# Where the folds of the next search and routing's small steps stand in VectorE's order: top-k attention into a mixture of experts

## The chip, the cores and the metric

The kernel runs on one core of one Trainium2 chip. The metric is the device time of one execution in microseconds, as the median of several runs. The engines are named as in the profile: PE is TensorE (PEld its weight loads), DVE is VectorE, ACT is ScalarE, POOL is GpSimd, SP is SyncE, which issues most DMAs.

## The reference

Attention for 8 batches of 8 heads with 576 tokens of 64 values, in which each query keeps only its 32 largest scores; then a mixture of 8 experts with one expert for each token.

```python
# attention: q, k, v are (8, 8, 576, 64) float32
scores = scale * np.matmul(q, k.transpose(0, 1, 3, 2))
kth = np.partition(scores, -32, axis=-1)[..., -32:-31]
scores = np.where(scores >= kth, scores, -1e9)
attn = np.exp(scores - max); attn = attn / (attn.sum(-1, keepdims=True) + 1e-09)
x = np.matmul(attn, v)          # then (B, H, S, D) -> (4608, 512)
# experts: w_gate (512, 8), w1 (8, 512, 1024), w2 (8, 1024, 512)
logits = x @ w_gate
expert = np.argmax(logits, axis=1)
gate = 1 / (exp(logits - max).sum(-1) + 1e-09)      # the probability of the chosen one
y = np.maximum(x @ w1[expert], 0) @ w2[expert]
out = gate[:, None] * y
```

## The kernel before

**Slots.** The work is 144 slots, 18 for each batch. A slot holds two tiles of 128 queries by 576 scores, lying side by side in one buffer `s` as 128 x 2 x 2 x 288. In `loop()` the order of PE, ACT and DVE is that of the program's text (a manual schedule for these three engines), and most POOL instructions are kept in program order by `in_turn`. PE multiplies the scores of slot i four slots ahead, ACT copies them to `s` three ahead (L306).

**The search.** For the 32nd largest score of a row DVE does not scan all 576 scores. It first folds them. `fold` makes h, the larger of the two halves (L313, 288 values for each of the two tiles), and l, the smaller (L315). `fold_on` folds h again: the larger quarter goes to `few` (L321), the smaller to `hl`. In `lists` (L350) the 8 largest of l and of the two halves of hl are put behind the 144 values of few. `search` then runs four rounds, in each of which MAX8 takes the next 8 largest of each tile (L372) and MATCH_REPLACE8 strikes them out (L382). What can have been missed is noted in `doubt` (L399), and a slow exact path behind the main loop would be taken if it mattered.

**When the folds come.** Slot i searches what was folded in slot i-1. Its text first folds s of slot i+1 to h and l, then runs its own search. `fold_on` for slot i+1 comes later, as a function `then` that `search` calls: in most slots ahead of the last round, in a quiet slot behind the second round's maxima. A slot is quiet if its number is between 1 and 47 and no rows, scatters or stores have been put on POOL (`k.crowded`). In a quiet slot hl is not made by DVE but by two integer operations of POOL (L326, L327: larger + smaller - larger).

**Behind the search.** ACT makes `low` from the 32nd value (L393), then w, a ReLU with a very steep slope, in two halves (`depths`, L409). POOL subtracts it from the scores (`less`, L418, two instructions of 128 x 576 that read s and w), and then makes `doubt`. ACT takes the exponential of w later in the slot (`weights`, L426). PE transposes w one slot later (`transposed`, L437, with ACT's copies L444), and multiplies by v in `outputs` (L474) when a unit of two heads is whole.

**Routing's small steps.** A batch's routing is spread over the slots behind it as generators: `divisors` (one reciprocal, L503, of what ACT has just put into rz), `choice` (L535 to L545), `places` (L570 to L579), `filled_up` and `table` (L642 to L677). Each yields after one small DVE instruction. They wait in the list `aside`. `tick()` runs one step of the first of them; `search` calls it in its third and fourth rounds, after each MAX8 and each MATCH_REPLACE8, which is six places a slot. `through(steps)` runs what is left of one before its result is needed. On POOL routing puts `logits` (L511 to L516), `rows` (L525, 128 x 640) and the scatters of finished rows to `x_rows` in DRAM (L590). `ending` is the generator that walks a unit through these places; `at_place(name)` moves it on.

**Experts.** Blocks of 128 rows of one expert are fetched (SP queue: rows L797, weights L789 and L791), and their matmuls (L942, L959) are cut into pieces that are mixed into the slots by a credit. What is left of them runs on PE when the slots are done. Before that `fill_up` writes empty rows behind each expert's last row, from the SBUF tile `blank`, which also fills nine blocks of `x_rows` at the start (L993).

Of the kernel before, what the change touches and what calls it, by code (L numbers as in the profile page):

```python
# [9 lines left out]
F32 = mybir.dt.float32  # L10
I32 = mybir.dt.int32
AF = mybir.ActivationFunctionType
ALU = mybir.AluOpType
# [31 lines left out]
def kernel(  # L45
# [47 lines left out]
    nc = tc.nc  # L93
    B, U, P, _ = qk.shape
    N, Dm = out.shape
    S = N // B
    E = moe_w_gate.shape[1]
# [6 lines left out]
    HF = S // 2  # L104
    QF = S // 4
# [5 lines left out]
    XW = Dm + 2  # L111
# [3 lines left out]
    CAP = N + P  # L115
# [125 lines left out]
    w1v = moe_w1.rearrange("e (dt p) f -> p e dt f", p=P)  # L241
    w2v = moe_w2.rearrange("e (ft p) d -> p e ft d", p=P)
    xv = x_rows.rearrange("(r p) w -> p r w", p=P)
    blank = const.tile([P, XW], F32, name="blank")
    nc.gpsimd.memset(blank[:, 0:Dm + 1], 0.0)
    nc.gpsimd.iota(blank[:, Dm + 1:XW].bitcast(I32), pattern=[[0, 1]], base=N, channel_multiplier=0)
    scattered, fetched, fills = [], [], []

    def groups(u):
# [4 lines left out]
    def in_turn(put):  # L254

        if not k.exact:
            tc.keep_in_program_order(put)
        return put
# [47 lines left out]
            lambda m=m, ps=ps: nc.scalar.copy(s[:, m, :, :], ps[:, :, 0:HF]) for m, ps in enumerate(got)  # L306
        ]

    def fold(s):

        f = SimpleNamespace()
        f.h = k.att.tile([P, 2, HF], F32, name="h", bufs=1)
        nc.vector.tensor_tensor(f.h, s[:, :, 0, :], s[:, :, 1, :], op=ALU.max)  # L313
        f.l = k.att.tile([P, 2, HF], F32, name="l")
        nc.vector.tensor_tensor(f.l, s[:, :, 0, :], s[:, :, 1, :], op=ALU.min)  # L315
        return f

    def fold_on(f, aside_too=False):

        f.few = k.att.tile([P, 2, LW], F32, name="few", bufs=3)  # L320
        nc.vector.tensor_tensor(f.few[:, :, 0:QF], f.h[:, :, 0:QF], f.h[:, :, QF:HF], op=ALU.max)  # L321
        hl = k.att.tile([P, 2, QF], I32, name="hl", bufs=1)
        f.hl, f.aside = hl[:, :, :].bitcast(F32), aside_too
        if aside_too:
            one, other, more = (a.bitcast(I32) for a in (f.h[:, :, 0:QF], f.h[:, :, QF:HF], f.few[:, :, 0:QF]))
            in_turn(nc.gpsimd.tensor_tensor(hl, one, other, op=ALU.add))  # L326
            in_turn(nc.gpsimd.tensor_tensor(hl, hl, more, op=ALU.subtract))  # L327
        else:
            nc.vector.tensor_tensor(f.hl, f.h[:, :, 0:QF], f.h[:, :, QF:HF], op=ALU.min)

    aside = []

    def tick():

        while aside:
            if next(aside[0], "end") != "end":
                return
            aside.pop(0)

    def through(steps):  # L340
        for _ in steps:
            pass
        if steps in aside:
            aside.remove(steps)

    def lists(f):

        for m in range(2):
            for j, away in enumerate((f.l[:, m, :], f.hl[:, m, 0:QF // 2], f.hl[:, m, QF // 2:QF])):
                nc.vector.max(out=f.few[:, m, QF + 8 * j:QF + 8 * j + 8], in_=away)  # L350

    def search(tiles, s, f, then=lambda: None, soon=False):

        m_all = range(2)
        tops = k.small.tile([P, 2, TOP_K], F32, name="tops", bufs=4)
        if k.exact:
            src = [s[:, m, :, :].rearrange("p j k -> p (j k)") for m in m_all]
            width = S
        else:
            src = [f.few[:, m, 0:QF] for m in m_all]  # L360
            width = LW
            if not f.aside:
                lists(f)
        scr = k.att.tile([P, 2, width], F32, name="scr", bufs=1)
        nbias = k.small.tile([P, 2], F32, name="nbias", bufs=3)
        R = TOP_K // 8

        for r in range(R):
            if r == R - 1 and not soon:
                then()  # L370
            for m in m_all:
                nc.vector.max(out=tops[:, m, r * 8:(r + 1) * 8], in_=src[m])  # L372
                if r > 1:
                    tick()
            if r == 1 and soon:
                then()
            if r == 0:
                in_turn(nc.gpsimd.tensor_scalar_mul(nbias, tops[:, :, 0], -scale))
            if r < R - 1:
                for m in m_all:  # L380
                    first = r == 0 and not k.exact
                    nc.vector.match_replace(  # L382
                        out=src[m] if first else scr[:, m, :], in_to_replace=tops[:, m, r * 8:(r + 1) * 8],
                        in_values=src[m], imm_value=NEG,
                    )
                    if r > 1:
                        tick()
                    src[m] = f.few[:, m, :] if first else scr[:, m, :]
                if first and f.aside:
                    lists(f)  # L390
        thr = tops[:, :, TOP_K - 1]
        low = k.small.tile([P, 2], F32, name="low", bufs=3)
        nc.scalar.activation(low, thr, AF.Copy, scale=STEEP)  # L393

        def doubts():
            n, i = tiles[0]
            at = n.b * U + n.u
            over = doubt[:, at:at + 2, 2 * NC, :] if tails(tiles) else doubt[:, at, 2 * i:2 * i + 2, :]
            k.last_pool = in_turn(nc.gpsimd.tensor_tensor(  # L399
                over, f.few[:, :, QF + 7:LW:8], _inner(thr, NL), op=ALU.subtract  # L400
            )).ins

        return low, nbias, doubts
# [583 lines left out]
    with fast:  # L987
        units = [(b, u) for b in range(B) for u in range(U)]
        unit.append(load_unit(*units[1]))
        for n in unit:  # L990
            load_values(n)
        for r in [e * CAP for e in range(E)] + [EMPTY * P]:
            nc.sync.dma_start(x_rows[r:r + P, :], blank)  # L993

        work = [(b, g) for b in range(B) for u in range(0, U, 2) for g in groups(u)]
        per_batch = len(work) // B
# [77 lines left out]
        def ending(b, u):  # L1074
# [15 lines left out]
            div = divisors(n)  # L1090
            next(div)
            aside.append(div)
            yield "products"
            next(out_steps)
            if b * U + u + 2 < len(units):
# [98 lines left out]
        def loop():  # L1194
# [5 lines left out]
                    step()  # L1200
            multiply(AHEAD)
            f_of[0] = fold(s_of[0])
            fold_on(f_of[0])
            for i, (b, g) in enumerate(work):
                tiles = tiles_of(i)
                u, tile = g[0]
                if tile == 0 and u % 2 == 0:
                    open_unit(tiles[0][0])
                if tails(tiles):
                    open_unit(tiles[1][0])  # L1210

                then, quiet = lambda: None, 0 < i < QUIET and not k.crowded
                if i + 1 < len(work):
                    f_of[i + 1] = fold(s_of[i + 1])
                    then = lambda: fold_on(f_of[i + 1], quiet)
                low, nbias, doubts = search(tiles, s_of[i], f_of.pop(i), then, quiet)
                k.crowded = False
                at_place("small")
                w_of[i] = depths(s_of[i], low)
                less(s_of.pop(i), w_of[i])  # L1220
                doubts()
                at_place("pool")
                at_place("relu")
                at_place("rows")
                put_stores()
                scatter(1)
                at = i % per_batch
                if at == FIRST and b:
                    rate = level(b) * PIECES / (U * NT)
                credit += rate * len(g)  # L1230
                room = left
                if b == B - 1 and at >= ARRIVED:
                    room -= KEEP
                    credit = room / (len(work) - i)
                share = {0: 0.5, 1: 1.2, 2: 1.6, 3: 0.5, 2 * NC: 1.4}[tile]
                now = max(0, min(int(credit * share + 0.5), room))
                credit -= now
                clock = i
                if i + AHEAD < len(work):
                    s_of[i + AHEAD], steps = scores(got_of.pop(i + AHEAD))  # L1240
                    for step in steps:
                        step()
                evacuate()
                at_place("turn")
                turns = turning(i - 1) if i else iter(())
                next(turns, None)
                part = min(BETWEEN, now - now // 2)
                rest = pieces(part)
                next(turns, None)
                rest = pieces(now - now // 2 - part + rest)  # L1250
                weights(tiles, w_of[i], nbias)
                next(turns, None)
                evacuate()
                if i + AHEAD + 1 < len(work):
                    multiply(i + AHEAD + 1)
                if tile == NC - 1:
                    end = ending(b, u)
                    late.append([end, next(end)])
                at_place("products")
                at_place("weights")  # L1260
                credit = min(credit + pieces(now // 2 + rest), 6 * rate)
# [149 lines left out]
```

## Time and profile before

| what | value |
| --- | --- |
| median of 3 runs | 1316.55 us (1310.98 to 1316.97) |
| the profiled execution's own time | 1312.35 us |
| its span, first to last instruction | 1310.7 us |
| mean granted TensorE clock | 0.969 |
| busy: PE, PEld | 1184.7 us (90%), 830.4 us (63%) |
| busy: DVE | 1064.8 us (81%), 4587 instructions |
| busy: ACT, POOL | 931.8 us (71%), 715.4 us (55%) |
| DMA | 220.95 MB, 169 GB/s over the span |

How to read the lines of the prediction. The busy slices cut the span into 40 equal parts, a digit being the busy share in tenths. A stretch has its bounds, its length, then busy time and number of instructions for PE, PEld, DVE, ACT and POOL, the granted clock, the share of the DMA engines and GB/s. A group has line, engine, operation, output<-input, shapes and count, then busy time in all and mean ns of one, then the engine's idle time ahead of it and what ended it. In the order of time a line begins with the start and the duration in us. "Waits" that the profile names are those on semaphores: an instruction that has been issued and stands still for another reason shows only as a long one.

### The profile page before, as it was taken

What the parts mean: (1) busy time and instruction counts of PE and PEld (TensorE: products, weight loads), DVE (VectorE), ACT (ScalarE), POOL (GpSimd) and SP (SyncE); (2) the same over time, 40 slices, a digit from 0 to 9 for tenths busy, and PEclk for the clock granted to TensorE, in tenths of its full rate; (3) what the DMA queues carried; (4) which work ended last, traced back from release to release, by engine and by line L of the source; (5) the groups of instructions that cost most, each with busy time, mean ns of one, the idle gap of its engine ahead of it and who ended that gap; (6) DMA issues with size and microseconds to landing.
All of it is one profiled execution on the core that took longest, in us unless ns stands there. A gap on an engine that the chain in (4) does not pass through costs nothing. (4 is left out here: it accounts for less than half of the span.)

```text
span 1310.7 us, 24598 instructions
## 1 busy us (share of the span) xinstructions
PE 1184.7 (90%) x7654; PEld 830.4 (63%) x7654; DVE 1064.8 (81%) x4587; ACT 931.8 (71%) x2136; POOL 715.4 (55%) x867
## 2 busy tenths in 40 slices
PE   5776676899889989999999999999999999999995
PEld 3443343666566556666666666767666777699973
DVE  7999999999999999999999999999999943000000
ACT  4888877898888888988888887898878851111210
POOL 4777766777755575658564745576558542000000
PEclk9778988999999999999999999999999999999998
DMA  5000112741474147534745554448454549986680
GB/s 150 30 30 30 31 38 90 278 165 39 142 267 137 47 158 283 175 110 159 291 174 183 161 217 174 165 149 283 147 199 158 209 161 295 386 298 213 219 286 19
DMA packets 98509, 220.95 MB, mean 169 GB/s; under 512 B 5181, under 2 KB 25917, under 8 KB 98368
## 3 DMA queue, kind: packets, MB, share of 16 engines
q1 hardware_dynamic: 91664, 199.02, 43.9%
q0 software_dynamic: 6416, 19.97, 4.3%
q8 instruction: 62, 1.02, 0.3%
q14 instruction: 79, 0.65, 0.2%
q10 hardware_dynamic: 288, 0.30, 0.1%
HBM read 195.88 MB, written 24.17 MB: 168 GB/s over the span
## 5 line engine op out<-in xcount | busy, mean ns | idle before, releaser
L418 POOL TENSOR_TENSOR w<-s,w 128x576 f32<-128x576 f32 x288 | 406.9, 1433 | 345.3 <-ACT w L409 345.2
L942 PE MATMUL ph<-xTs,w 128*128 128x128 f32 x2112 | 259.6, 276 | 3.3 <-ACT xTs L839 3.0
L942 PEld LDWEIGHTS ph<-xTs,w 128*128 128x128 f32 x2112 | 248.0, 192 | 22.5 <-issue 18.7
L959 PE MATMUL py<-w,hT 128*128 128x512 f32 x528 | 248.2, 599 | 3.6 <-ACT hT L947 3.5
L426 ACT ACTIVATE w<-w,nbias 128x576 f32<-128x576 f32 x288 | 224.1, 793 | 2.9 <-POOL w L418 2.1
L409 ACT ACTIVATE w<-s,low 128x576 f32<-128x576 f32 x288 | 207.7, 768 | 4.7
L299 PE MATMUL sc<-qkb 64*128 64x288 f32 (+1 forms) x1280 | 196.8, 459 | 9.5 <-ACT s L306 5.1
L437 PE MATMUL wTm<-turn,w 128*128 128x128 f32 x1152 | 167.7, 284 | 27.2 <-ACT oT L476 12.9
L437 PEld LDWEIGHTS wTm<-turn,w 128*128 128x128 f32 x1152 | 130.1, 144 | 84.0 <-issue 34.6
L306 ACT COPY s<-sc 128x576 f32<-128x576 f32 x288 | 168.8, 639 | 9.0 <-PE sc L299 9.0
L372 DVE MAX8 tops<-scr 128x8 f32<-128x168 f32 x576 | 165.2, 314 | 0.0
L1290 DVE CAST any_i<-pd 1x1 int32<-1x1 f32 x1 | 0.1, 147 | 201.9 <-PE pd L1288 201.9
L444 ACT COPY wT<-wTm 128x512 f32<-128x512 f32 x256 | 139.0, 603 | 23.8 <-PE wTm L437 23.7
L372 DVE MAX8 tops<-few 128x8 f32<-128x144 f32 (+1 forms) x576 | 151.0, 300 | 0.0
L299 PEld LDWEIGHTS sc<-qkb 64*128 64x128 f32 (+1 forms) x1280 | 105.4, 188 | 69.9 <-issue 32.3
L474 PE MATMUL po<-wT,vb 128*64 128x288 f32 x1024 | 148.9, 436 | 0.0
L959 PEld LDWEIGHTS py<-w,hT 128*128 128x128 f32 x528 | 91.7, 191 | 88.4 <-issue 82.7
L857 POOL DMA_INDIRECT out_dram<-y,xg x37 | 38.9, 1052 | 171.3 <-ACT y L968 86.0
L350 DVE MAX8 few<-l 128x8 f32<-128x288 f32 x288 | 126.9, 441 | 0.0
L474 PEld LDWEIGHTS po<-wT,vb 128*64 128x64 f32 x1024 | 72.1, 146 | 72.3 <-issue 22.1
L313 DVE TENSOR_TENSOR h<-s 128x576 f32<-128x576 f32 x144 | 109.1, 758 | 2.3 <-ACT s L306 2.0
L315 DVE TENSOR_TENSOR l<-s 128x576 f32<-128x576 f32 x144 | 109.0, 757 | 0.0
(190 smaller groups left out, 1701.1 us busy)
## 6 DMA issues: line engine op xcount, KB each, us to landing
w<-in_moe_w_dram SPq DMA_DIRECT2D x74, 2048.0 KB, 9.1
qkb<-in_qk_dram SPq DMA_DIRECT2D x31, 608.0 KB, 4.0
vb<-in_v_dram SPq DMA_DIRECT2D x32, 320.0 KB, 3.2
xg<-x_rows SPq DMA_DIRECT2D x37, 257.0 KB, 9.5
x_rows<-blank SPq DMA_DIRECT2D x13, 257.0 KB, 6.5
x_rows<-blank POOLq DMA_DIRECT2D x4, 257.0 KB, 9.0
x_rows<-x,posi POOLq DMA_INDIRECT x40, 3.5
out_dram<-y,xg POOLq DMA_INDIRECT x37, 4.1
```

Of the source, the lines that this page charges most:

```text
L299: nc.tensor.matmul(ps[rows, j, 0:HF], n.q[d, cols], n.k[d, keys], start=True, stop=True)
L306: lambda m=m, ps=ps: nc.scalar.copy(s[:, m, :, :], ps[:, :, 0:HF]) for m, ps in enumerate(got)
L350: nc.vector.max(out=f.few[:, m, QF + 8 * j:QF + 8 * j + 8], in_=away)
L372: nc.vector.max(out=tops[:, m, r * 8:(r + 1) * 8], in_=src[m])
L409: nc.scalar.activation(w[:, m, :], s[:, m, :, :].rearrange("p j k -> p (j k)"), AF.Relu, scale=-STEEP, bias=low[:, m:m + 1],)
L418: k.last_pool = in_turn(nc.gpsimd.tensor_tensor(w[:, m, :], s[:, m, :, :].rearrange("p j k -> p (j k)"), w[:, m, :], op=ALU.subtract)).ins
L426: nc.scalar.activation(w[:, m, :], w[:, m, :], AF.Exp, scale=scale, bias=nbias[:, m:m + 1], accum_out=n.z[:, c:c + 1])
L437: nc.tensor.transpose(pm[:, c * P:(c + 1) * P], w[:, m, first:first + P], ident)
L444: nc.scalar.copy(wT[:, :, m, q], pm4)
L474: nc.tensor.matmul(po[r, 0:HF], n.v[:, c, r], rhs, start=(c == 0), stop=(c == KC - 1))
L942: nc.tensor.matmul(ph[:, f, :], n.w1[:, 0, dt, fc * P:(fc + 1) * P], n.xT[:, dt, :], start=(dt == 0), stop=(dt == DT - 1),)
L959: nc.tensor.matmul(py, hT[:, f, :], n.w2[:, 0, f, :], start=(f == 0), stop=(f == FT - 1))
```

## The change

All four folds of slot i+1 now stand at the beginning of slot i, ahead of the search: h, l, few, hl. In quiet slots only h and l do; few and POOL's hl stay behind the second round's maxima. The calls of `tick` leave the rounds: in a slot that is not quiet there is one behind each of the four folds, in a quiet slot one behind h and one behind l, and in every slot there are two behind the last round. A `divisors` generator rests (list `rested`) until the first last round after it was made, so that its reciprocal isn't run between the folds. `tick` takes the next generator that isn't resting. Since hl of the next slot is now written before that of this one is read, hl gets two buffers; the room comes from `blank`, which moves to DRAM and is written once at the start from a row buffer of the experts.

```diff
@@ blank
-    blank = const.tile([P, XW], F32, name="blank")
-    nc.gpsimd.memset(blank[:, 0:Dm + 1], 0.0)
-    nc.gpsimd.iota(blank[:, Dm + 1:XW].bitcast(I32), pattern=[[0, 1]], base=N, channel_multiplier=0)
+    blank = dram.tile([P, XW], F32, name="blank")
@@ fold, fold_on
-    def fold(s):
+    def fold(s, aside_too=False, between=lambda: None):
-        f = SimpleNamespace()
+        f = SimpleNamespace(aside=aside_too)
         f.h = k.att.tile([P, 2, HF], F32, name="h", bufs=1)
         nc.vector.tensor_tensor(f.h, s[:, :, 0, :], s[:, :, 1, :], op=ALU.max)
+        between()
         f.l = k.att.tile([P, 2, HF], F32, name="l")
         nc.vector.tensor_tensor(f.l, s[:, :, 0, :], s[:, :, 1, :], op=ALU.min)
+        between()
+        if not aside_too:
+            fold_on(f, between)
         return f
-    def fold_on(f, aside_too=False):
+    def fold_on(f, between):
         f.few = k.att.tile([P, 2, LW], F32, name="few", bufs=3)
         nc.vector.tensor_tensor(f.few[:, :, 0:QF], f.h[:, :, 0:QF], f.h[:, :, QF:HF], op=ALU.max)
-        hl = k.att.tile([P, 2, QF], I32, name="hl", bufs=1)
...
+        between()
+        f.hl_i = k.att.tile([P, 2, QF], I32, name="hl")
+        f.hl = f.hl_i[:, :, :].bitcast(F32)
+        if not f.aside:
             nc.vector.tensor_tensor(f.hl, f.h[:, :, 0:QF], f.h[:, :, QF:HF], op=ALU.min)
+            between()
+            return
...
@@ tick
-    aside = []
+    aside, rested = [], []
     def tick():
-        while aside:
-            if next(aside[0], "end") != "end":
+        for steps in list(aside):
+            if steps in rested:
+                continue
+            if next(steps, "end") != "end":
                 return
-            aside.pop(0)
+            aside.remove(steps)
@@ search
         for r in range(R):
-            if r == R - 1 and not soon:
-                then()
             for m in m_all:
                 nc.vector.max(out=tops[:, m, r * 8:(r + 1) * 8], in_=src[m])
-                if r > 1:
-                    tick()
-            if r == 1 and soon:
-                then()
             if r == 0:
                 in_turn(nc.gpsimd.tensor_scalar_mul(nbias, tops[:, :, 0], -scale))
+            elif r == 1:
+                then()
...
-                    if r > 1:
-                        tick()
...
+        rested.clear()
+        for _ in m_all:
+            tick()
         thr = tops[:, :, TOP_K - 1]
@@ the start
-        for r in [e * CAP for e in range(E)] + [EMPTY * P]:
-            nc.sync.dma_start(x_rows[r:r + P, :], blank)
+        empty = k.mlp.tile([P, 1, XW], F32, name="xg", bufs=4)[:, 0, :]
+        nc.gpsimd.memset(empty[:, 0:Dm + 1], 0.0)
+        nc.gpsimd.iota(empty[:, Dm + 1:XW].bitcast(I32), pattern=[[0, 1]], base=N, channel_multiplier=0)
+        for to in [x_rows[r:r + P, :] for r in [e * CAP for e in range(E)] + [EMPTY * P]] + [blank]:
+            nc.sync.dma_start(to, empty)
@@ ending
             aside.append(div)
+            rested.append(div)
@@ loop
             f_of[0] = fold(s_of[0])
-            fold_on(f_of[0])
...
-                then, quiet = lambda: None, 0 < i < QUIET and not k.crowded
+                then = lambda: None
                 if i + 1 < len(work):
-                    f_of[i + 1] = fold(s_of[i + 1])
-                    then = lambda: fold_on(f_of[i + 1], quiet)
-                low, nbias, doubts = search(tiles, s_of[i], f_of.pop(i), then, quiet)
+                    f_of[i + 1] = fold(s_of[i + 1], 0 < i < QUIET and not k.crowded, tick)
+                    if f_of[i + 1].aside:
+                        then = lambda: fold_on(f_of[i + 1], lambda: None)
+                low, nbias, doubts = search(tiles, s_of[i], f_of.pop(i), then)
```

More of the change, by code (lines that the diff above doesn't have):

```diff
@@ L307, in scores @@
         ]
-    def fold(s):
-        f = SimpleNamespace()
+    def fold(s, aside_too=False, between=lambda: None):
+        f = SimpleNamespace(aside=aside_too)
         f.h = k.att.tile([P, 2, HF], F32, name="h", bufs=1)
         nc.vector.tensor_tensor(f.h, s[:, :, 0, :], s[:, :, 1, :], op=ALU.max)
+        between()
         f.l = k.att.tile([P, 2, HF], F32, name="l")
         nc.vector.tensor_tensor(f.l, s[:, :, 0, :], s[:, :, 1, :], op=ALU.min)
+        between()
+        if not aside_too:
+            fold_on(f, between)
         return f
-    def fold_on(f, aside_too=False):
+    def fold_on(f, between):
         f.few = k.att.tile([P, 2, LW], F32, name="few", bufs=3)
         nc.vector.tensor_tensor(f.few[:, :, 0:QF], f.h[:, :, 0:QF], f.h[:, :, QF:HF], op=ALU.max)
-        hl = k.att.tile([P, 2, QF], I32, name="hl", bufs=1)
[L323 to L329, printed above, removed]
-    aside = []
+        between()
+        f.hl_i = k.att.tile([P, 2, QF], I32, name="hl")
+        f.hl = f.hl_i[:, :, :].bitcast(F32)
+        if not f.aside:
+            nc.vector.tensor_tensor(f.hl, f.h[:, :, 0:QF], f.h[:, :, QF:HF], op=ALU.min)
+            between()
+            return
+        one, other, more = (a.bitcast(I32) for a in (f.h[:, :, 0:QF], f.h[:, :, QF:HF], f.few[:, :, 0:QF]))
+        in_turn(nc.gpsimd.tensor_tensor(f.hl_i, one, other, op=ALU.add))
+        in_turn(nc.gpsimd.tensor_tensor(f.hl_i, f.hl_i, more, op=ALU.subtract))
+    aside, rested = [], []
     def tick():
-        while aside:
-            if next(aside[0], "end") != "end":
+        for steps in list(aside):
+            if steps in rested:
+                continue
+            if next(steps, "end") != "end":
                 return
-            aside.pop(0)
+            aside.remove(steps)
     def through(steps):
@@ L342, in through @@
             pass
-        if steps in aside:
-            aside.remove(steps)
+        for some in (aside, rested):
+            if steps in some:
+                some.remove(steps)
     def lists(f):
@@ L350, in lists, with search @@
                 nc.vector.max(out=f.few[:, m, QF + 8 * j:QF + 8 * j + 8], in_=away)
-    def search(tiles, s, f, then=lambda: None, soon=False):
+    def search(tiles, s, f, then=lambda: None):
         m_all = range(2)
```

## The prediction

> **What bounds the kernel now.** I read the page's busy slices first, then the busy time by stretch, then the groups by shape, then single slots in order of time on VectorE (DVE) and GpSimd (POOL).
>
> ```profile
> PE   5776676899889989999999999999999999999995
> DVE  7999999999999999999999999999999943000000
> ACT  4888877898888888988888887898878851111210
> ```
>
> DVE is full up to about 1058 us; behind it lie some 250 us of TensorE (PE) alone. So a slot's length is set by DVE.
>
> ```profile
> 516.00:700.00 184.00, 179.94 (x1197) 122.50 (x1198) 182.42 (x769) 155.81 (x361) 114.55 (x133) 1.00 0.52 184
> 700.00:900.00 200.00, 197.57 (x1352) 138.38 (x1352) 199.64 (x848) 170.45 (x396) 125.61 (x147) 1.00 0.54 188
> ```
>
> The columns after the length are PE, weight loads, DVE, ACT, POOL. From 516 us on PE too is busy 98% by its modelled ends, so a faster DVE could find PE in its way there.
>
> ```profile
> L313 DVE TENSOR_TENSOR h<-s 128x576 f32<-128x576 f32 x144 | 109.1, 758 | 2.3 <-ACT s L306 2.0 <-POOL hl L326 0.2
> L321 DVE TENSOR_TENSOR few<-h 128x288 f32<-128x288 f32 x144 | 80.8, 561 | 0.0
> L329 DVE TENSOR_TENSOR hl<-h 128x288 f32<-128x288 f32 x114 | 53.3, 467 | 0.0
> L418 POOL TENSOR_TENSOR w<-s,w 128x576 f32<-128x576 f32 x288 | 406.9, 1433 | 345.3 <-ACT w L409 345.2
> ```
>
> Two folds of one shape differ: hl 467 ns, few 561. The source line of few shows 430/441/1621 ns as least, median and longest. The tail is where a POOL instruction is running. One such place, DVE's answer and then POOL's:
>
> ```profile
> 960.68 1.30 DVE L321 TENSOR_TENSOR few<-h 128x288 f32<-128x288 f32 x1
> 961.91 1.65 DVE L329 TENSOR_TENSOR hl<-h 128x288 f32<-128x288 f32 x1
> 963.48 0.32 DVE L372 MAX8 tops<-scr 128x8 f32<-128x168 f32 x1
> ...
> 960.26 2.98 POOL L418 TENSOR_TENSOR w<-s,w 128x576 f32<-128x576 f32 x2 [2.62 <-ACT w L409]
> ```
>
> few stands still through the first half of `less`, hl through the second. Unhindered they step 0.37 us each; here (961.91-960.68) + (963.48-961.91) = 2.80 us, 2.06 us more.
>
> [...] the scans with one input run through `less` at 0.21 to 0.44 us[...] the free few took 430 to 450, h 727 to 758.
>
> **Where the folds go.** In 112 of the 142 slots followed (those without the quiet path), few and hl leave their place before the last round, about 5.7 us into a slot, and follow l at +1.31 us. Nothing is added: the free slot is 6.92 us before and after. What changes is which POOL instruction they meet. The free slot in order: last max, h at 0, l at +0.66, l's end +1.40; ACT makes low (+0.11) and w's first half (done +1.12); POOL's `less` starts at +1.20, has to wait some 0.06 us for l, and runs in two halves to +2.67 and +4.04. In the old place few and hl come after it; in the new one few is issued at +1.31, with `less` already waiting for 0.11 us. So all hangs on one thing: **does a waiting POOL instruction get in between two back-to-back folds?** The trace has that between h and l:
>
> ```profile
> 598.22 0.73 DVE L313 TENSOR_TENSOR h<-s 128x576 f32<-128x576 f32 x1
> 598.87 0.74 DVE L315 TENSOR_TENSOR l<-s 128x576 f32<-128x576 f32 x1
> 598.75 0.94 POOL L378 TENSOR_SCALAR nbias<-tops 128x2 f32<-128x2 f32 x1
> ...
> 567.94 0.74 DVE L313 TENSOR_TENSOR h<-s 128x576 f32<-128x576 f32 x1
> 568.59 0.75 DVE L315 TENSOR_TENSOR l<-s 128x576 f32<-128x576 f32 x1
> 568.47 0.28 POOL L378 TENSOR_SCALAR nbias<-tops 128x2 f32<-128x2 f32 x1
> ```
>
> Both times nbias is issued 0.12 us ahead of l. At 598 it waits for h and l (0.94 us); at 568 it gets in (0.28 us). I went through all such pairs (h-l, few-hl). Where DVE's durations are in their short form (h 726 to 731 ns), POOL lost 10 of 10 that began over 50 ns after the first fold. In the long form (h 732 and up, which is how slots look after a fold has been held) it won 8 of 8; of seven that began earlier six lost. In the trace 73 of the 112 slots are in the long form, 39 in the short. I take it that `less`, starting 0.55 us into l, wins in long-form slots and loses in short ones.
>
> **The sum.** If it wins: few lets hl be issued about 0.24 us past the first half's end (as at 961.91), at +2.91 in place of +1.68: 1.23 us. The second half is then already waiting behind a fold that was held, and wins again, as at 960 and at 1029 us: hl costs 1.21 us. Together 2.44 us a slot, and a held fold leaves the long form behind it. In 31 long-form slots `less` comes before +1.38 now. In the other 42 ACT is late (low up to 4.6 us behind the max) and `less` comes after the folds; but each slot made longer gives ACT time to catch up, so I count half of them: 52 slots, 52 x 2.44 = 127 us. Off it goes what few and hl lose now in these slots, 14.8 + 2.9 = 17.7 us above 440 ns each, and some of the small steps' loss: those of routing above 0.3 us lose 17.4 us in the DVE-bound part (L642, L648, L675, L539 held up to 1.3 us, one L659 4.2 us). Between the folds and behind the last scan they meet `less` too, so I take 5 us. Net 127-18-5 = +104 us.
>
> **The other edits.** The steps' number stays (six places a slot: four between folds, two behind the last scan; four in quiet slots, whose remainder is run together before it is needed). The reciprocal L503 is kept for the last scan: there one wait of 5.7 us for ACT is known, and at +0.66 us many more would come, so resting it costs nothing. Where a one-input step (a reduction) stands between two folds it opens the pair for POOL even in the short form; some 3 slots a batch. few's buffer is now written a slot's length earlier: `doubts` of two slots before must have read it. It follows `less`, which ends at +4.04 in a free slot and past +6.9 in 10 of 142; cost 0 to 5 us, I take 0. SBUF for a second hl is made by moving `blank` to DRAM: a tenth start-up DMA (issue about 0.56 us on SP, behind the first loads; the next SP issue, at 22.45, is 8 us later, so nothing) and eight fills at 1096 to 1101 us that read DRAM. The row loads behind them already wait (L797, 44.0 us in nine waits) with PE busy 49.7 of 50 us; if they land later PE's one gap of 0.31 us grows: 0 to 3 us, I take 1. That those fills could gain I exclude: nothing is taken off any queue. POOL's side: where DVE keeps its turn, `less` starts 0.75 us later; ACT's exp (L426) starts mostly 1 us or more after `less` ends and waits only 2.1 us in all, so it is covered.
>
> 1312.35 us (the profiled execution: span 1310.7 and 1.65 around it) + 105 = 1417; the median shown is 4.2 us above that execution, so I write **1420**. Its own range is 1365 (31 slots only, less 25) to 1560 (all 112).
>
> **Rivals.** *Faster: DVE keeps its turn.* If a back-to-back fold holds off POOL whatever the form, as it does in the short one, the folds meet nothing and the 17.7 us plus half of the steps' 17.4 go. Against it stand the eight wins; for it, that `less` comes within 0.11 us of few and that held folds, which bring the long form, become fewer. After 516 us PE leaves only 542-533 = 9 us, and rows (L525, 1.31 us, which holds few a dozen times now) slides against the next h. So -15 us of the two: about 1300. It decides where fewer than 10 slots are blocked (25/2.44). *No change:* PE, at 98%, sets the slot and ACT follows it, or some ten blocked slots eat the gain: 1313 to 1318. *Half as bad:* only few is held and the second half loses to hl: 52 x 1.23 - 23 = +41, 1355. *The change doesn't do what it says* would need the compiler to move few back; DVE's order is by hand, so hardly.
>
> **How the numbers follow.** Slower 0.63 (full blocking 0.48, half 0.15), no change 0.09, faster 0.28. 0.5% (6.6 us) is about what can be told from no change here. To leave out no more than 2 in 10 the range must reach into the faster case and most of the blocked one: 1290 to 1530.
>
> **What would show it.** Right: the few and hl rows well above their 561 and 467 ns, near 1.2 and 1.2 us on the mean of blocked slots; slots of 9.3 to 9.5 us; the small steps' rows near 0.2 us; `less` at +1.20 with a second half of 1.6 us. Wrong: few and hl at 440 ns with `less` starting near +2.0 us and nbias around 1 us: then DVE kept its turn, and what is left is whether DVE or PE ends the slot.

## The result: slower by 3.6%, and the profile after

The changed kernel takes 1357.04 us in the median of six runs (1356.51 to 1369.05), the kernel before 1312.62 in six on the same chip: ratio 1.0361, interval 1.0332 to 1.0389, or +44 us. Its profiled execution took 1356.51 us, with a span of 1354.9. Line numbers of the kernel after lie a few above those of before: h is L311, l L314, few L323, hl L328, `less` L422, the places' first step (`pos`) L574, the table's `step_all` L656.

The busy slices and the busy time by stretch of the kernel after (columns as before: PE, weight loads, DVE, ACT, POOL, clock, DMA share, GB/s):

```profile
PE   5777676998989788998999999989999999999995
DVE  8999999999999899999998999899989964000000
```

```profile
516.00:700.00 184.00, 171.05 (x1134) 118.85 (x1134) 180.97 (x747) 147.33 (x341) 113.92 (x123) 0.98 0.54 190
700.00:900.00 200.00, 193.94 (x1313) 134.78 (x1309) 190.15 (x803) 163.36 (x380) 120.38 (x136) 0.99 0.52 179
```

DVE still ends the slots, but its row now has four slices of 8 among the nines, and it runs out a little later: the two slices behind them read 6 and 4 in place of 4 and 3. From 700 to 900 us it is busy 190.15 us, not 199.64, and gets through 803 instructions, not 848: it does less and also stands idle. The last h starts at 1091.2 us in place of 1046.4 (+44.8); from there to the end of the span it is 263.7 us in place of 264.4. So the whole loss lies in the slots.

The groups by shape (busy in all, mean ns, idle ahead of it):

```profile
L311 DVE TENSOR_TENSOR h<-s 128x576 f32<-128x576 f32 x144 | 109.8, 762 | 3.9 <-ACT s L304 3.4 <-POOL hl L332 0.2
L314 DVE TENSOR_TENSOR l<-s 128x576 f32<-128x576 f32 x144 | 117.2, 814 | 0.0
L323 DVE TENSOR_TENSOR few<-h 128x288 f32<-128x288 f32 x144 | 74.7, 519 | 0.1
L328 DVE TENSOR_TENSOR hl<-h 128x288 f32<-128x288 f32 x114 | 61.0, 535 | 0.0
...
L656 DVE TENSOR_TENSOR step_all<-done,full 1x7 f32<-1x7 f32 x8 | 8.4, 1056 | 0.0
```

The prediction looked for few and hl near 1.2 us. few fell from 561 to 519 ns, hl rose from 467 to 535: nearly a tie. The last line is a step of 7 elements that takes 1056 ns on the mean. Before, it took 143, and `pos`, the other step that matters below, waited only at the end (1.9 us):

```profile
L652 DVE TENSOR_TENSOR step_all<-done,full 1x7 f32<-1x7 f32 x8 | 1.1, 143 | 0.0
L570 DVE TENSOR_TENSOR pos<-rank,oh 128x40 f32<-128x40 f32 x8 | 1.4, 179 | 1.9 <-ACT blocks L1124 1.9
```

**Slot by slot.** Cut at the starts of h and compared by number, from slot 1 on:

| slots | before, us | after, us |
| --- | --- | --- |
| 88 plain ones (no step of routing but the reciprocal) | 631.0 | 633.1 |
| 26 quiet ones | 174.6 | 175.1 |
| 29 with steps of routing | 236.8 | 279.3 |

The folds' new place, which the prediction priced at +109 us, moved the plain slots by 2.1 us. The small steps, priced at -5, cost 42.5. Of those, DVE's idle time is 25.3 us (from 0.4 to 25.7); the steps' own time above their free one grew by 6.2, l's by 5.2, few's and hl's by 3.8.

**A plain slot of after**, in order of time (start, duration), DVE's folds and then POOL's `less`:

```profile
377.92 0.73 DVE L311 TENSOR_TENSOR h<-s 128x576 f32<-128x576 f32 x1
378.58 0.74 DVE L314 TENSOR_TENSOR l<-s 128x576 f32<-128x576 f32 x1
379.25 0.44 DVE L323 TENSOR_TENSOR few<-h 128x288 f32<-128x288 f32 x1
379.62 0.44 DVE L328 TENSOR_TENSOR hl<-h 128x288 f32<-128x288 f32 x1
...
379.12 3.58 POOL L422 TENSOR_TENSOR w<-s,w 128x576 f32<-128x576 f32 x2 [4.00 <-ACT w L413]
```

`less` is issued 0.13 us ahead of few, as foreseen, but few and hl step the free 0.37 us each. POOL's first half stands until hl has been read (it ends at 381.34, 1.36 us behind hl's successor at 379.98) and costs DVE nothing. It was so in 30 of the 35 plain slots in which `less` was waiting when few came, and in 18 of the 22 of those in the long form, where the prediction gave POOL every one. In the other five (at 150, 368, 420, 510 and 652 us) both folds were held, at the price predicted: at 368 us few took 1.66 us, hl 1.65, and the slot 9.43 against a free 6.92. In four of these five h or l had itself been held just before (h 0.82 to 0.83 us, or l 1.36), in none of the 30; at 420 us neither had.

**Slots with routing's steps.** What DVE waits for on semaphores (engine, waiting, on whom: us, times, longest):

```profile
DVE pos L574 <- ACT blocks L1132: 21.9, 7, 4.5
DVE mx L539 <- POOL lg L518: 8.4, 6, 5.6
```

One of these waits in order of time (the bracket is the idle time ahead and what ended it):

```profile
1013.07 0.74 DVE L311 TENSOR_TENSOR h<-s 128x576 f32<-128x576 f32 x1
1018.25 0.20 DVE L574 TENSOR_TENSOR pos<-rank,oh 128x40 f32<-128x40 f32 x1 [4.44 <-ACT blocks L1132]
1018.36 0.75 DVE L314 TENSOR_TENSOR l<-s 128x576 f32<-128x576 f32 x1
...
1016.69 1.26 PE L563 MATMUL rank<-oh,ones 128*128 128x40 f32 x10
...
1017.99 0.17 ACT L1130 COPY run<-rank 128x8 f32<-128x8 f32 x1 [2.47 <-PE rank L563]
1018.05 0.16 ACT L1132 ACTIVATE blocks<-rank 1x8 f32<-1x8 f32 x1
```

`pos` reads the PSUM tile `rank`. It stands second in the slot now, with l, few, hl and the whole search behind it on DVE. The releaser named, ACT's `blocks`, is only the last of three: ACT itself stood 2.47 us for PE, whose last `rank` matmul ends at 1017.95, 4.89 us into the slot. ACT's two readings of the same tile come between: `run` starts at 1017.99, `blocks` ends at 1018.21, and `pos`, which doesn't need their results, starts at 1018.25, 0.30 us behind the matmul's end. In the six such slots of the loop `rank` ends 1.86 to 4.90 us behind h, and `pos` loses 20.0 us in all; the seventh wait, 1.85 us at the end, was there before. Before, `pos` stood at +4.87 to +5.25, in the third round, with `rank` done by +4.32 at the latest: no wait in the loop.

And a slot of the table's steps, DVE and then POOL:

```profile
887.77 0.15 DVE L652 TENSOR_TENSOR left<-full,done 1x8 f32<-1x8 f32 x1
...
888.30 0.43 DVE L328 TENSOR_TENSOR hl<-h 128x288 f32<-128x288 f32 x1
888.66 1.36 DVE L656 TENSOR_TENSOR step_all<-done,full 1x7 f32<-1x7 f32 x1
...
887.44 3.94 POOL L422 TENSOR_TENSOR w<-s,w 128x576 f32<-128x576 f32 x2 [3.92 <-ACT w L413]
```

`less` has waited since 887.44, and the step of 7 elements behind hl stands through its first half. The place behind hl is just where the waiting POOL instruction gets in, as in the plain slot above.

### The profile page after: what moved, and what is told of

It is laid out like the page before. It is cut to its first block, busy times and chain, and to the rows that moved or that the text cites. A ratio compares the mean times of both kernels' runs of the same rounds, so it can differ in the third digit from the quotient of the medians.

```text
span 1354.9 us, 24561 instructions
## 1 busy us (share of the span) xinstructions
PE 1205.4 (89%) x7654; PEld 844.8 (62%) x7654; DVE 1085.1 (80%) x4587; ACT 932.8 (69%) x2136; POOL 753.0 (56%) x867
## 5 line engine op out<-in xcount | busy, mean ns | idle before, releaser
L422 POOL TENSOR_TENSOR w<-s,w 128x576 f32<-128x576 f32 x288 | 458.3, 1611 | 320.7 <-ACT w L413 320.6
L946 PE MATMUL ph<-xTs,w 128*128 128x128 f32 x2112 | 264.2, 279 | 2.2 <-ACT xTs L843 2.2
L946 PEld LDWEIGHTS ph<-xTs,w 128*128 128x128 f32 x2112 | 252.7, 195 | 21.5 <-issue 18.1
L963 PE MATMUL py<-w,hT 128*128 128x512 f32 x528 | 251.5, 605 | 2.5 <-ACT hT L951 2.3
L297 PE MATMUL sc<-qkb 64*128 64x288 f32 (+1 forms) x1280 | 200.5, 463 | 9.2 <-ACT s L304 5.1
L377 DVE MAX8 tops<-scr 128x8 f32<-128x168 f32 x576 | 159.1, 314 | 0.0
L478 PE MATMUL po<-wT,vb 128*64 128x288 f32 x1024 | 153.3, 447 | 0.0
L314 DVE TENSOR_TENSOR l<-s 128x576 f32<-128x576 f32 x144 | 117.2, 814 | 0.0
L311 DVE TENSOR_TENSOR h<-s 128x576 f32<-128x576 f32 x144 | 109.8, 762 | 3.9 <-ACT s L304 3.4
```

Of the source, the lines that this page charges most:

```text
L297: nc.tensor.matmul(ps[rows, j, 0:HF], n.q[d, cols], n.k[d, keys], start=True, stop=True)
L422: k.last_pool = in_turn(nc.gpsimd.tensor_tensor(w[:, m, :], s[:, m, :, :].rearrange("p j k -> p (j k)"), w[:, m, :], op=ALU.subtract)).ins
L478: nc.tensor.matmul(po[r, 0:HF], n.v[:, c, r], rhs, start=(c == 0), stop=(c == KC - 1))
L946: nc.tensor.matmul(ph[:, f, :], n.w1[:, 0, dt, fc * P:(fc + 1) * P], n.xT[:, dt, :], start=(dt == 0), stop=(dt == DT - 1),)
L963: nc.tensor.matmul(py, hT[:, f, :], n.w2[:, 0, f, :], start=(f == 0), stop=(f == FT - 1))
```

## The experiments

Two theories on the loss. **S**: the steps' new places cost all of it, the folds nothing. Its rival is the prediction's own: the folds in front of `less` cost it. Beside them **T**, on why the folds kept their turn: a waiting `less` doesn't get in between DVE instructions with two inputs that follow one another, but does where one with one input stands between. The ratio is always to the kernel before on the same chip.

**e1: the folds alone.**

```diff
@@ search (after)
             nc.vector.max(out=tops[:, m, r * 8:(r + 1) * 8], in_=src[m])
+            if r > 1:
+                tick()          # likewise behind each MATCH_REPLACE8
...
-        for _ in m_all:
-            tick()
@@ ending
-            rested.append(div)
@@ loop
-  f_of[i + 1] = fold(s_of[i + 1], 0 < i < QUIET and not k.crowded, tick)
+  f_of[i + 1] = fold(s_of[i + 1], 0 < i < QUIET and not k.crowded)
```

> The folds as in the changed kernel, routing's steps in the third and fourth rounds as before. Theory S (the steps between the folds cost the time: the 29 slots that hold steps went from 236.8 to 279.3 us, the 88 plain ones from 631.0 to 633.1): the loss goes, 1308 to 1320 us. Rival F (few and hl at their new place meet less): most of the loss stays, 1340 us or more.

Measured: 1314.60 us (1310.05 to 1319.36), ratio 1.0016 [1.0006, 1.0026]. Its groups:

```profile
L323 DVE TENSOR_TENSOR few<-h 128x288 f32<-128x288 f32 x144 | 74.9, 520 | 0.4
L328 DVE TENSOR_TENSOR hl<-h 128x288 f32<-128x288 f32 x114 | 61.4, 539 | 0.0
```

The two rows are those of after, and 42 of the 44 us are gone. Slots with steps take 235.6 us, under the 236.8 of before. (Its profiled execution took 1319.06 us, 4.5 over the median; plain slots take 638.4 in it, 7.4 over before.) The prediction's theory falls as the cause of the loss. The folds' move brings no gain either.

**e2: the steps alone.** The kernel before, few and hl at their old place, `blank` left in SBUF; two steps behind h, two behind l, two behind the last round.

```diff
@@ fold (before)
         nc.vector.tensor_tensor(f.h, s[:, :, 0, :], s[:, :, 1, :], op=ALU.max)
+        between()
+        between()
...
         nc.vector.tensor_tensor(f.l, s[:, :, 0, :], s[:, :, 1, :], op=ALU.min)
+        between()
+        between()
@@ search
-                if r > 1:
-                    tick()      # likewise behind MATCH_REPLACE8
...
+        rested.clear()
+        for _ in m_all:
+            tick()
@@ ending
+            rested.append(div)
```

> few and hl where they were before; routing's steps at the slot's beginning, two behind h and two behind l, and two behind the last scan; blank in SBUF as before. Theory S: the loss is there without the folds being moved, 1340 to 1365 us. Rival F: at most 10 us over the kernel before, 1312 to 1323 us.

Measured: 1361.24, ratio 1.0375 [1.0358, 1.0392]. Slots with steps take 285.6 us, plain ones 633.5. The waits show the same stall:

```profile
DVE pos L576 <- ACT blocks L1131: 22.1, 7, 4.3
```

The steps' new places alone make the whole loss. S holds from both sides.

**e3: the places' steps rest.** After, and `places` waits for the last round as the reciprocal does.

```diff
             steps = places(r, x)
             aside.append(steps)
+            rested.append(steps)
```

> The changed kernel, but the generator of places rests as that of divisors does, so that its first step (pos) is not run between the folds of the slot after it was made. Theory S, part 'a step waits for ACT at a slot's beginning': pos's 21.9 us of idle go, and what DVE would wait elsewhere stays away, 1330 to 1340 us. If the wait is hidden by what ACT or PE needs anyway: 1350 us or more.

Measured: 1332.50, ratio 1.0157 [1.0140, 1.0173], 24.5 us under after. The wait of `pos` falls from 21.9 to 1.9 us (that at the end), and slots with steps from 279.3 to 245.4:

```profile
DVE pos L574 <- ACT blocks L1133: 1.9, 1, 1.9
```

One line of code takes away over half of the loss. Of those 33.9 us plain slots give back 11.2 (633.1 to 644.3): DVE waits 8.8 us for s (3.4 in after), and more of h and hl is held.

**e4: all six steps behind the last round.** After, with `fold` called without `tick`, and `for _ in range(6)` there.

> The changed kernel with no step between the folds: all six behind the last scan. Theory S: waits for ACT and POOL go, and no step opens the pairs of folds for less; 1308 to 1325 us. Rival F: 1340 us or more. If the steps' nearness to each other is what costs: above 1330 us, with the steps' rows longer than 0.2 us.

Measured: 1334.28, ratio 1.0166 [1.0149, 1.0183]: above the band of S, and where the steps' nearness to each other was to show. Slots with steps take 247.5 us, 10.7 over before, and plain ones 640.3, 9.3 over, much as in the profile of e1. Standing in a row there, steps wait for one another (some 0.1 us a slot), and the last ones are held by `less` for 1.1 to 1.4 us. So both places cost more than the old one: with single steps among the scans of the last rounds these slots took 236.8 us.

**e7: places and choice rest.** e3, and `rested.append(r.steps)` for `choice`.

> The changed kernel, with the generators of places and of choice resting. e3 (places alone) gave 1332.5 us. Theory S: choice's slots (41, 59, 77 took 9.7 to 11.9 us in the changed kernel against 7.2 to 7.6 before, 95, 113 and 131 about the same) come down to 8 us: 5 to 10 us less than e3, 1322 to 1328 us. If choice's loss only moves to where DVE is held later in the slot: 1330 to 1336 us.

Measured: 1340.10, ratio 1.0204 [1.0187, 1.0221], worse than e3 and above both bands. The slots with steps gain 5 us more (240.5), but in plain ones few and hl are held for 12 us each, and they take 653.6. It may be that what is taken from one slot shifts POOL's `less` in those behind it; no run shows this by itself.

**e5: a one-input instruction between l and few.** e1 and, ahead of few, a reciprocal of 128 x 10 on a tile that nobody else uses: 114 more instructions.

```diff
@@ fold (e1)
         if not aside_too:
+            nc.vector.reciprocal(spare_in, spare_in)
             fold_on(f, between)
```

> The kernel of e1 (folds together, steps in the rounds) with one more DVE instruction in each slot that is not quiet: a reciprocal of 128x10, one SBUF input, between l and few. Theory T (POOL cannot get in while two-input instructions follow each other without a break, whatever form the durations have): the break lets less in where it waits at +1.20, so few and hl are held 1.2 us each in some 40 to 60 slots: 1390 to 1450 us. Rival (DVE goes first in any case): 112 x 0.10 us = 11 us more than e1, 1322 to 1330 us.

Measured: 1390.10, ratio 1.0570 [1.0539, 1.0601], 75.5 us over e1. The 114 reciprocals step 0.13 us each, some 14 us. The other 61 are the regime that the prediction described:

```profile
431.20 0.74 DVE L316 TENSOR_TENSOR l<-s 128x576 f32<-128x576 f32 x1
431.87 0.20 DVE L319 RECIPROCAL spare_in<-spare_in 128x10 f32<-128x10 f32 x1
432.00 1.53 DVE L326 TENSOR_TENSOR few<-h 128x288 f32<-128x288 f32 x1
433.45 1.65 DVE L331 TENSOR_TENSOR hl<-h 128x288 f32<-128x288 f32 x1
...
431.75 3.04 POOL L427 TENSOR_TENSOR w<-s,w 128x576 f32<-128x576 f32 x2 [4.00 <-ACT w L418]
```

`less` is issued 0.12 us ahead of the reciprocal and runs through it; few stands through the rest of the first half, hl through the second: a slot of 9.41 us (most of the held ones take 9.34). few was held in 41 slots, hl in 36, in runs of slots one behind the other. T holds here for `less` and a one-input instruction, though not always: of the 42 slots in which `less` was waiting when the reciprocal came, few was held in 34.

**e6, e8, e11, e12: a two-input instruction there.** Four fillers in the same place: e6 takes the maximum of 128 x 8 with itself; e8 is e6 with a wait, long fulfilled, on h; e11 reads h, as few does, 128 x 2 x 4; e12 is e6 with 224 in place of 8.

```diff
@@ fold (e1)
+   e6:  nc.vector.tensor_tensor(spare_in[:, 0:8], spare_in[:, 0:8], spare_in[:, 0:8], op=ALU.max)
+   e8:  put = (as e6);  tc.add_manual_dep(put.ins, first.ins.name, WAIT)      # first makes h
+   e11: nc.vector.tensor_tensor(spare_in[:, :, 0:4], f.h[:, :, 0:4], f.h[:, :, QF:QF + 4], op=ALU.max)
+   e12: nc.vector.tensor_tensor(spare_in, spare_in, spare_in, op=ALU.max)     # 224 wide
```

> As e5, but the instruction between l and few has two SBUF inputs (a maximum of 128x8 with itself). Theory T: no break, so its own 0.1 us in 112 slots is all, 1320 to 1332 us. Rival (any third instruction, or the time few comes later, lets less in): as e5, 1390 us or more.

> As e6 (a maximum of 128x8 between l and few, 1343 us, itself held 1.38 us in most plain slots), but this instruction waits on a semaphore, for h, which is long done when its turn comes. Theory W (in the long form a two-input instruction that has no wait loses its turn to a waiting POOL instruction, and one that has a wait keeps it; few has two waits, hl, l and e6's filler have none): the filler is no longer held, and few still waits for POOL's semaphore, so 1318 to 1328 us. Rival (the size or the place of the filler lets less in): as e6, 1338 us or more.

> As e6, but the maximum of 128x8 between l and few reads h, in the same three-dimensional form as few, and waits for h as few does. If what is read (h, just written) or the wait on it is what lets few keep its turn: the row of this instruction has a mean near 0.16 us and few is free, 1318 to 1328 us. If its shortness is what loses the turn: some 24 of its instructions are held 1.2 us or more as in e6, 1338 us or more.

> As e6, but the maximum between l and few is 128x224 with itself[...], no wait. If shortness loses the turn: this one keeps it, its row has a mean near 0.39 us, and the time is e1's plus 112 x 0.30 us, 1343 to 1352 us. If any unrelated instruction between l and few loses it: over 20 of them held 1.2 us, 1370 us or more.

Measured: e6 1343.48, ratio 1.0228 [1.0207, 1.0250]; e8 1347.38, 1.0264 [1.0227, 1.0301]; e11 1367.45 and e12 1343.94, one run each beside 1312.31 for the kernel before. The filler's own group, of e6 and then of e12:

```profile
L319 DVE TENSOR_TENSOR spare_in<-spare_in 128x8 f32<-128x8 f32 x114 | 51.5, 452 | 0.0
```

```profile
L319 DVE TENSOR_TENSOR spare_in<-spare_in 128x224 f32<-128x224 f32 x114 | 49.1, 431 | 0.0
```

e6 fell between the expectations: few and hl stayed free (4 and 5 slots held), but the filler itself took 1.38 us in 24 slots (not in most, as the expectation of e8 has it). So two inputs aren't enough to keep the turn, and T is too narrow. e8 and e11 tested whether a wait (theory **W**: what carries a wait keeps its turn), or reading h, makes the difference between the filler and few: it doesn't (24 and 45 fillers held). e12 tested length: in the same place a filler of 224 was held in 5 slots, with 379 ns as its median. Of the slots in which `less` was waiting when the filler came, it was held in 21 of 36 in e6, 19 of 33 in e8, 42 of 55 in e11 and 4 of 40 in e12. A long two-input instruction mostly keeps its turn there, a short one often loses it.

**e10: waits on the other folds.** e1, with fulfilled waits on l (for the last maximum) and on hl (for l), in case the wait is what lets few keep its turn.

> The kernel of e1 (1314.6 us), with a wait on an earlier DVE instruction, already done, given to l (on the last maximum) and to hl (on l) where all four folds stand together. Theory W: hl's 7.3 us of being held in plain slots go, part of l's too; h's stay, 1306 to 1314 us. Rival (waits don't decide): as e1, 1312 to 1318 us; if each wait costs DVE a break of 0.05 to 0.1 us: 1325 us or more.

Measured: 1315.60, ratio 1.0020 [1.0009, 1.0031]: e1 again. The wait isn't it.

**c1: few and hl behind the last scan.** The kernel before, with `then()` called behind the rounds, so that few, hl, h, l stand in a row.

> The kernel before with few and hl one round later, behind the last scan, so that few, hl, h, l follow each other; all else as before. If the folds in one run are worth the few's loss of 14 us: 1300 to 1308 us. If less, held until the run's end, holds ACT and PE in turn, or rows (L525) holds few at its new place: 1311 to 1322 us.

Measured: 1407.39, ratio 1.0700 [1.0660, 1.0740]: a miss, far from the 1300 to 1322 expected.

```profile
L315 DVE TENSOR_TENSOR l<-s 128x576 f32<-128x576 f32 x144 | 201.5, 1399 | 0.0
L313 DVE TENSOR_TENSOR h<-s 128x576 f32<-128x576 f32 x144 | 117.0, 812 | 13.8 <-ACT s L306 1.7 <-ACT w L409 0.5
```

h has one buffer, so each h must wait for hl, the instruction just ahead, to end: DVE stands 0.104 us there each time, the most of the 13.8 us. After that gap l, which is as long as a fold gets, took 1.96 us in 77 slots, and l lost 94.2 us in all. That a wait on the instruction directly ahead cost l its turn is what the times suggest; it wasn't tried by itself.

What stays open is the rule of the pair itself. Length decides for the filler in e12 (held in 5 slots, against 24 in e6), but not everywhere: in the table slot shown above, the steps at 887.77 and at 888.21 (8 elements) kept their turn while `less` was waiting, and only the one behind hl lost it. And where h had been slightly held (0.82 us) and `less` was waiting, few and hl lost theirs. No version beat the kernel before; e1, the folds alone, is nearest.

## Why the prediction was right on the side and wrong on the cause

It said slower, 1420 us, +104 on the profiled execution; measured was +44 for another reason than the one it gave. That it came out slower, and inside its range of 1290 to 1530, is luck: the term that made it slower measured almost nothing, and one that it took for a gain made the loss.

- **"I take it that `less` … wins in long-form slots and loses in short ones": the step that failed.** It made 52 blocked slots. There were five plain ones in which the folds lost to a `less` already waiting; in 30 `less` lost to them. The term of +109 us (127 less 17.7) measured +2.1 in the plain slots, and e1 as a whole +1.9. The wins that it counted were real, but between h and l they are those of `nbias` (five times, 2 elements a partition), `logits` (twice, 40) and `rows` (once, 640, behind an h that was held), and it carried them over to `less`. Eight instances, mostly of other and smaller instructions, were no ground for blocking every long-form slot. (By its own bound, h of 732 ns and more, the trace of before has 69 of these, not 73; that changes little. Nor did the long form mark a slot behind a held fold alone: in that trace it stood in 36 of the 39 slots behind one, h or l above 0.8 us or few or hl above 0.5, and in 61 of the 104 others.)
- **The price, "together 2.44 us a slot", was right**: 9.43-6.92 = 2.51 us at 368 us, and 9.34 us in most of e5's held slots. e5 shows that the regime exists, that it spreads from slot to slot, and that one small instruction with one input calls it up.
- **"Of routing above 0.3 us lose 17.4 us … I take 5 us": wrong in sign.** It asked only which POOL instruction each step would meet. It didn't ask when each step's input is ready. `pos` reads what PE makes in the same slot, and the trace of before had it: `rank` ended up to 4.32 us behind h, and its reader stood at +4.87. Moved to +0.7 it was bound to wait 20 us in six slots; `mx`, waiting for POOL's logits, adds 2.8. The prediction did this reckoning for the reciprocal (5.7 us known, hence resting) and for nothing else.
- **"Where a one-input step stands between two folds it opens the pair … some 3 slots a batch": right, and left without a price.** l, few and hl lost 9.0 us more in slots with steps. Behind `mx`, a reduction, l took 1.69 us in five of the seven slots that have it there, all to `rows`, and behind `den` few took 1.55 in two, to `less`. In these seven h was in the long form (732 to 757 ns); that a step opens the pair in the short form too was the author's estimate and isn't shown. And some of l's part comes behind `pos`, for which DVE had stood still. Not foreseen is that the step behind hl is itself held: `step_all` 1056 ns on the mean.
- **Costs taken at nothing.** few's earlier buffer (0 to 5), `blank` in DRAM and its fills (0 to 3, taken as 1): from the last h to the end 0.7 us less than before, so nothing is seen. That `less` starts 0.75 us later is covered: it starts near +2.0 and plain slots aren't longer for it. The reciprocal at rest costs nothing that shows.
- **The rivals.** *Faster* had the right mechanism for the folds (DVE keeps its turn), but not its gain: few's held time fell from 14.0 to 6.4 us in the plain slots, hl's rose from 1.6 to 8.2, h and l lost some 2 us more. That PE would end the slots instead isn't shown: h waits 3.4 us for s in all. *Half as bad* lands at 1355, but by a mechanism (few held, hl free) that no plain slot shows, and only three with steps (at 436, 596 and 873 us).
- **What would show it.** "few and hl at 440 ns with `less` starting near +2.0 us … then DVE kept its turn" was its sign of being wrong, and the trace gave it in the 30 slots, though not in the means over all.

## What to carry to other kernels

Before a small instruction is moved forward in an engine's order, look up when its last input is ready, in the same stage of the trace: `pos`, which holds its engine for 0.1 us, stood there for up to 4.5 us, and everything behind it on VectorE waited too. When the profile names a releaser, follow it one step further: here ACT was named, and PE was late. Where VectorE's two-input instructions stand together and a two-input GpSimd one is waiting, put no small instruction between them (e5 took 75 us more than e1, e6 some 29) and let none wait for the one just ahead (c1, in which l lost 94 us; the wait wasn't tried by itself); standing together was by itself no gain here (e1, ratio 1.0016). And judge who gets in by instances of the same two instructions, not by others of like kind.

## What the runs showed of the hardware that was not expected

- A waiting `less` (128 x 576, two SBUF inputs) let two further VectorE folds pass and started when hl had been read, in 30 of 35 plain slots; in four of the five others h or l had been held just before. In the 30 `less` was issued ahead of few by 0.10 to 1.27 us (median 0.16) and still went last.
- A reciprocal that steps 0.13 us, put between two folds, cost 75.5 us over 114 uses (e5 against e1), 0.66 us each, four fifths of it beyond its own step.
- A two-input instruction of 8 elements a partition took 1.38 us in 24 of 114 places (e6), where one of 224 was held in 5 (e12).
- A wait for the VectorE instruction directly ahead showed as 0.104 us of idle time, and the fold behind the one that waited, l, took 1.96 us in 77 of 144 slots (c1). That the one brought the other wasn't tried by itself.
